# Batch 0 valued by half tiles, low-rank products in pairs, and one batch's keys and queries loaded sooner in a fused attention and mixer kernel

## Chip, cores, metric

The kernel runs on one core of one Trainium2 chip. The metric is the device time of one launch in microseconds (us). The span of a profile is about 1.75 us shorter than the time of the same execution; where milestones are compared below, they count from the start of the span.

## The reference, cut to what matters

```python
# 8 batches, 8 heads, 576 tokens, head size 64; window 64; rank 32
scores = q @ k^T / 8, kept where 0 <= i - j < 64
x = softmax(scores) @ v                        # (8, 576, 512), heads side by side
u = x + (x^T @ U @ V)^T                        # U: 576 x 32, V: 32 x 576, over tokens
out = u + relu(u @ w_ch1) @ w_ch2              # 512 -> 2048 -> 512, "expert products"
```

## The kernel before

The tokens of all batches are cut into nine chunks of 512. A chunk is a list of 32 slots of TensorE work: 16 first products (psA) and 16 quarters of second products (psU), 0.86 us each. The attention of later batches is put between those slots; a table says after which slot each piece comes. Batch 0 has nothing to hide behind, so it runs alone in the first 22 us. From batch 2 on, K and Q are transposed by DMA (`TX`), and each batch's V, K and Q are loaded by DMAs that POOL issues. A copy of one element, `held`, makes POOL wait for an earlier transpose before it issues more.

```python
def PV(t):                                     # batch 0: values of token tile t
    def f():
        xr = ps_big.tile([P, 2, CH], FP32, name="xr", tag="big")
        for h in range(H):
            for blk in blks:
                values(xr[r0 : r0 + W, h // 4, cols], h, blk)
        nc.vector.reciprocal(out=rcp[lo:hi], in_=xv[:, :, :, D:VW])
        nc.vector.tensor_tensor(out=x[lo:hi, t, :, :]..., in0=xv[:, :, :, 0:D], in1=rcp..., op=ALU.mult)
    return f

def UM(ts):                                    # low-rank U product
    for t in ts:
        if t < 4:                              # tile t into column group t
            nc.tensor.matmul(hh["ps"][t * R : (t + 1) * R, :], ub[odd][:, t, :], xt,
                             start=True, stop=False)
            continue
        for g in range(4):                     # last tile, a quarter of the columns to each group
            nc.tensor.matmul(hh["ps"][g * R : (g + 1) * R, cols], ub[odd][:, t, :], xt[:, cols],
                             start=False, stop=True)
    # ... cut: hh["sb"] <- hh["ps"] on ACT

def VM(ts):                                    # low-rank V product, all 128 rows, one per tile
    nc.tensor.matmul(ps[0][:, n, :], vrep[:, off : off + P], hh["sb"][:], start=True, stop=True)
    # ... cut: u = psv + x on DVE, one per tile

def loads(b, *tiles):
    for t in tiles:
        nc.gpsimd.tensor_copy(out=held[:], in_=qfs[(b + 1) % 2][0:1, t * HP * P : t * HP * P + 1])
        if t == tiles[0] and len(tiles) > 1:
            load_v(b + 1)
    for _ in load_kq(b + 2, False):
        pass
# ... cut
if 1 < b and b + 1 < B:
    load_v(b + 1)
# ... cut
slots[20].append(lambda: loads(1, 2, NT - 1))  # hold, V of batch 2, hold, K and Q of batch 3
```

The softmax here doesn't subtract the row's maximum and nothing guards it: scores larger than these inputs give would overflow.

Of the kernel before, what the change touches and what calls it, by code (L numbers as in the profile page):

```python
# [16 lines left out]
def kernel(  # L17
# [11 lines left out]
    nc = tc.nc  # L29
# [192 lines left out]
    def load_rest():  # L222
# [3 lines left out]
        shift_low(0, nc.gpsimd.tensor_copy, 0)  # L226
        for t in range(1, 3):
            shift_low(0, nc.gpsimd.tensor_copy, t)
        load_w1(1024, 2048)
        for g in range(2):  # L230
            spread_v(g, nc.gpsimd.tensor_copy)
# [17 lines left out]
    def attention(b, spare=False):  # L249
# [34 lines left out]
        def TK(j):  # L284
            def f():
                copy = nc.vector.tensor_copy if spare and j == 2 else nc.scalar.copy
                copy(out=place_of(kt, j), in_=tr(kb, j))
            return f

        def TQ(j):  # L290
            def f():
                copy = nc.vector.tensor_copy
                copy(out=place_of(qt, j), in_=tr(qb, j, b == 1))  # L293
            return f
# [114 lines left out]

        def PV(t):  # L410
            def f():
                blks = [bl for bl in (2 * t - odd, 2 * t + 1 - odd) if 0 <= bl < NB]
                lo = W if (odd and t == 0) else 0
                hi = W if (not odd and t == NT - 1) else P

                xr = ps_big.tile([P, 2, CH], FP32, name="xr", tag="big")
                for h in range(H):
                    for blk in blks:
                        r0 = ((blk + odd) % 2) * W
                        cols = slice((h % 4) * VW, (h % 4 + 1) * VW)  # L420
                        values(xr[r0 : r0 + W, h // 4, cols], h, blk)
                xv = xr[lo:hi, :, 0 : 4 * VW].rearrange("p a (h e) -> p a h e", e=VW)
                rcp = wk_pool.tile([P, 2, 4, 1], FP32, name="rcp", tag="rcp")
                nc.vector.reciprocal(out=rcp[lo:hi], in_=xv[:, :, :, D:VW])
                nc.vector.tensor_tensor(
                    out=x[lo:hi, t, :, :].rearrange("p (a h) d -> p a h d", a=2),
                    in0=xv[:, :, :, 0:D],
                    in1=rcp[lo:hi].to_broadcast([hi - lo, 2, 4, D]),
                    op=ALU.mult,
                )  # L430
# [60 lines left out]
        def UM(ts):  # L491
            def f():
# [5 lines left out]
                for t in ts:  # L498
                    xt = x[:, t, :, :].rearrange("p h d -> p (h d)")
                    if t < 4:  # L500
                        nc.tensor.matmul(  # L501
                            hh["ps"][t * R : (t + 1) * R, :], ub[odd][:, t, :], xt,
                            start=True, stop=False,
                        )
                        continue

                    for g in range(4):
                        cols = slice(g * P, (g + 1) * P)
# [47 lines left out]
        def HT(dcs):  # L556
            def f():
                for dc in dcs:
                    nc.tensor.matmul(
                        bank(dc),  # L560
                        hh["sb"][:, dc * P : (dc + 1) * P],
                        vrep[:, W : W + CH],
# [11 lines left out]
        def VM(ts):  # L574
            ps = {}

            def up():
                ps[0] = ps_big.tile([P, 2, CH], FP32, name="psv", tag="big")
                for n, t in enumerate(ts):
                    off = t * P + (0 if odd else W)  # L580
                    nc.tensor.matmul(  # L581
                        ps[0][:, n, :], vrep[:, off : off + P], hh["sb"][:], start=True, stop=True
                    )

            def add(n):
                def f():
                    t = ts[n]
# [3 lines left out]
                    )  # L591
                    if g not in u_tiles:
                        u_tiles[g] = u_pool.tile([P, DM], BF16, name="un")
                    nc.vector.tensor_tensor(  # L594
                        out=u_tiles[g][rs, :],
                        in0=ps[0][rs, n, :],
                        in1=x[rs, t, :, :].rearrange("p h d -> p (h d)"),
# [4 lines left out]
            return [up] + [add(n) for n in range(len(ts))]  # L602
# [26 lines left out]
        pcs["PV"] = [PVA] if not spare else [PV(t) for t in range(NT)]  # L629
        pcs["U"] = [UM((t,)) for t in range(NT)] if spare else [UM(tuple(range(NT)))]  # L630
        if spare:
            pcs["XT"] = [XT(t, range(NDC - 1)) for t in range(NFULL)]
# [4 lines left out]
        else:  # L637
            def whole(ts):
                fs = VM(ts)
                return lambda: [f() for f in fs]  # L640

            pcs["V"] = [whole(ts) for ts in ((0, 1), (2, 3), (4,))]
# [7 lines left out]
    def mlp(c):  # L650
# [3 lines left out]
        def ch1(*ids):  # L654
            def f():
# [5 lines left out]
                for dc in range(NDC):  # L661
# [260 lines left out]
```

## Time and profile before

| | before |
|---|---|
| time, median of the runs at hand when predicting | 313.64 us (313.63 to 318.27) |
| span of the profile | 313.4 us, granted clock 1.00 |
| TensorE busy | 306.1 us |
| first expert product | 21.97 us |
| longest wait of TensorE for a DMA | 1.00 us, before batch 3's scores |

The head of the page of the kernel before. The first line gives busy time, share of the span and instructions of each engine; the others give the busy share in tenths in forty slices of the span.

```profile
PE 306.1 (98%) x2875; PEld 150.9 (48%) x2875; DVE 162.2 (52%) x298; ACT 108.6 (35%) x174; POOL 101.3 (32%) x133
PE   8899999999998999999999999999999999999996
DMA  7999999999999999999999999965100520020012
```

TensorE is never long idle after batch 0. The line of the DMA engines is as full as that of TensorE over the first 25 slices, some 200 us. (It counts the time for which packets are under way; summed over the engines that can exceed 1, so it does not say that no more bytes could pass.)

The list of waits of TensorE, kernel before (engine, line, tile, what it waited for: us in total, times, longest):

```profile
PE low L340 <- DMA qf<-qr: 1.0, 1, 1.0
```

The timeline of SyncE's DMA queue, kernel before: the first and the last of the ten transposing DMAs of batch 3 (start, us of issuing), and the timeline of TensorE at the wait:

```profile
74.62 1.20 SPq L299 DMA_TRANSPOSE kf<-kr  x1
...
89.60 1.37 SPq L299 DMA_TRANSPOSE qf<-qr  x1
```

```profile
93.08 1.03 PE L663 MATMUL psA<-uTc,w1b 128*128 128x512 bf16 x4
...
95.11 0.19 PE L340 MATMUL low<-qf,kf 64*64 64x64 bf16 x1 [1.00 <-DMA qf<-qr]
```

TensorE had finished the slot's expert product by about 94.1 us and stood until the last transposed Q had landed.

The timeline of DVE in batch 0, kernel before: the first and the last of five pairs of reciprocal and multiply.

```profile
15.71 0.21 DVE L424 RECIPROCAL rcp<-xr 128x8 f32<-128x8 f32 x1 [2.34 <-PE xr L402]
15.95 0.69 DVE L425 TENSOR_TENSOR xs<-xr,rcp 128x512 bf16<-128x512 f32 x1
...
19.22 0.20 DVE L424 RECIPROCAL rcp<-xr 64x8 f32<-64x8 f32 x1
19.46 0.68 DVE L425 TENSOR_TENSOR xs<-xr,rcp 64x512 bf16<-64x512 f32 x1
```

Then come ACT's copy of the U product and TensorE's first expert product, kernel before:

```profile
20.48 0.65 ACT L516 CAST hh<-psh 128x256 bf16<-128x256 f32 x2 [1.83 <-PE psh L509]
...
21.97 1.89 PE L663 MATMUL psA<-uTc,w1b 128*128 128x512 bf16 x8
```

The chain of waits of the kernel before, around batch 3's low-rank products (start, us, what). `pshh` is the U product, `psv` the V product.

```profile
110.38 0.33 PE pshh L501 x4
110.71 0.06 PE pshh L509 x4
110.77 0.97 PE psA L663 x4
111.74 0.86 PE psU L687 x4
112.60 0.43 PE psv L581 x2
```

The U product takes 0.39 us. The four expert matmuls behind it take 0.97 us instead of 0.86. Five V products take 5 x 0.216 = 1.08 us.

### The profile page before, as it was taken

Reading aid. Unit: us, or ns where it says so; the run is one execution under the profiler, and the core shown is the slowest. Engines: PE = TensorE matmul, PEld = TensorE weight load, DVE = VectorE, ACT = ScalarE, POOL = GpSimd, SP = SyncE. Lnnn points to the kernel's source line nnn. Section 1 sums busy time; section 2 is a strip of 40 time slices with the busy share of each in tenths; the row PEclk is TensorE's granted clock in tenths of the full one; section 3 lists DMA queues with packets and bytes.
Section 4 is the critical chain, followed back from the end, with each engine's and each line's share of the span. In section 5 each row is a group of like instructions: output and inputs, shape, how many; then the busy total and the mean of one; then the engine's idle time right before and its main releaser. Section 6 shows DMA issues by size and latency. Waiting matters only on the chain.

```text
span 313.4 us, 6904 instructions
## 1 busy us (share of the span) xinstructions
PE 306.1 (98%) x2875; PEld 150.9 (48%) x2875; DVE 162.2 (52%) x298; ACT 108.6 (35%) x174; POOL 101.3 (32%) x133
## 2 busy tenths in 40 slices
PE   8899999999998999999999999999999999999996
PEld 7554554544444544454445444544454444444443
DVE  4475468337756843684358445744574443016011
ACT  3655660467027520533043404440345003301500
POOL 8683263159439346426543571000000000000000
PEclk9999999999999999999999999999999999999999
DMA  7999999999999999999999999965100520020012
GB/s 104 164 208 208 206 168 146 129 180 192 121 153 200 159 152 147 193 140 159 175 174 156 170 156 158 178 99 131 67 2 2 134 84 2 14 86 33 2 61 73
DMA packets 156495, 39.87 MB, mean 127 GB/s; under 512 B 145040, under 2 KB 151440, under 8 KB 156464
## 3 DMA queue, kind: packets, MB, share of 16 engines
q0 software_dynamic: 104720, 18.88, 82.5%
q1 hardware_dynamic: 51744, 20.55, 39.2%
q8 instruction: 22, 0.36, 0.4%
q14 instruction: 9, 0.07, 0.1%
HBM read 37.97 MB, written 9.44 MB: 151 GB/s over the span
## 4 chain that ended last, share of the span: by engine, by line
PE 81%; DMA 13%; POOL 3%; DVE 2%; issue 1%; SPq 0%; POOLq 0%
PE psU L687 36%; PE psA L663 36%; DMA qr<-in_q_dram 4%; DMA vB<-in_v_dram 4%; DMA vA<-in_v_dram 3%; PE psv L581 2%; PE xw L402 2%; PE sc L340 2%; DMA qf<-qr 2%; DVE xs L469 1%; POOL vA L134 1%; PE pshh L501 1%; POOL kr L116 1%; PE tpu L613 0%; POOL vrep L220 0%
## 5 line engine op out<-in xcount | busy, mean ns | idle before, releaser
L687 PE MATMUL psU<-w2b,c 128*128 128x512 bf16 (+2 forms) x592 | 131.3, 373 | 0.1
L663 PE MATMUL psA<-uTc,w1b 128*128 128x512 bf16 x576 | 131.0, 379 | 0.0
L687 PEld LDWEIGHTS <-c 128*128 128x128 bf16 x592 | 56.6, 98 | 64.8 <-issue 0.5
L663 PEld LDWEIGHTS <-w1b 128*128 128x128 bf16 x576 | 54.2, 98 | 64.4 <-issue 1.8
L675 ACT ACTIVATE c<-psA 128x512 bf16<-128x512 f32 x84 | 50.1, 597 | 88.8 <-PE psA L663 88.2
L697 DVE TENSOR_TENSOR osb<-psU,un 128x512 f32<-128x512 f32 (+2 forms) x37 | 24.9, 677 | 76.7 <-PE psU L687 76.3
L673 DVE TENSOR_SCALAR c<-psA 128x512 bf16<-128x512 f32 x60 | 41.3, 689 | 25.5 <-PE psA L663 25.5
L594 DVE TENSOR_TENSOR un<-psv,xs 128x512 bf16<-128x512 f32 (+1 forms) x40 | 25.5, 685 | 22.9 <-PE psv L581 22.7
L134 POOL DMA_DIRECT2D vA<-in_v_dram x32 | 28.6, 909 | 17.3 <-PE psU L687 3.1
L360 ACT ACTIVATE pts<-sc 128x1024 bf16<-128x1024 f32 x32 | 31.3, 1028 | 2.7 <-PE sc L340 2.7
L125 POOL DMA_DIRECT2D kr<-in_k_dram x30 | 25.8, 860 | 10.1 <-DMA vA<-in_v_dram 3.5
L125 POOL DMA_DIRECT2D qr<-in_q_dram x30 | 25.9, 864 | 8.9 <-DMA w2b<-in_moe_w_ch_dram 3.2
L393 ACT ACTIVATE ptl<-low 128x256 bf16<-128x256 f32 x6 | 2.3, 384 | 64.4 <-PE high L340 64.4
L366 DVE TENSOR_TENSOR pts<-pts,maskA 128x1024 bf16<-128x1024 bf16 x28 | 19.1, 682 | 1.1 <-ACT pts L360 1.1
L469 DVE TENSOR_TENSOR xs<-xw,rcw 128x896 bf16<-128x896 f32 x14 | 15.3, 1092 | 0.5
L340 PEld LDWEIGHTS <-kf 64*64 64x64 bf16 x704 | 9.9, 107 | 8.8 <-issue 8.2
L846 POOL COPY held<-qf 1x1 bf16<-1x1 bf16 x6 | 1.1, 178 | 39.4 <-DMA qf<-qr 39.4
L581 PE MATMUL psv<-hh,vrep 128*128 128x512 bf16 x40 | 12.5, 379 | 0.0
L402 PEld LDWEIGHTS <-pts 128*64 128x64 bf16 x512 | 10.0, 110 | 4.7 <-issue 3.7
L340 PE MATMUL sc<-qf,kf 64*64 64x128 bf16 (+1 forms) x608 | 11.6, 212 | 0.6 <-DVE qf L293 0.6
L134 POOL DMA_DIRECT2D vB<-in_v_dram x8 | 7.2, 901 | 5.9 <-DMA qr<-in_q_dram 2.5
L616 ACT COPY uTc<-tpu 128x512 bf16<-128x512 bf16 x9 | 5.3, 586 | 10.8 <-PE tpu L613 10.8
(108 smaller groups left out, 171.2 us busy)
## 6 DMA issues: line engine op xcount, KB each, us to landing
out_dram<-osb SPq DMA_DIRECT2D x35, 256.0 KB, 5.0
vA<-in_v_dram POOLq DMA_DIRECT2D x32, 128.0 KB, 13.1
kr<-in_k_dram POOLq DMA_DIRECT2D x24, 128.0 KB, 8.7
qr<-in_q_dram POOLq DMA_DIRECT2D x24, 128.0 KB, 8.9
w2b<-in_moe_w_ch_dram POOLq DMA_DIRECT2D x4, 512.0 KB, 15.7
vB<-in_v_dram POOLq DMA_DIRECT2D x8, 128.0 KB, 13.7
w1b<-in_moe_w_ch_dram POOLq DMA_DIRECT2D x2, 512.0 KB, 10.9
w1b<-in_moe_w_ch_dram POOLq DMA_DIRECT2D x1, 1024.0 KB, 10.0
```

What stands on the lines that cost most here:

```text
L125: nc.gpsimd.dma_start(out=dst[0:rows, t, :, :], in_=src[b, :, t * P : t * P + rows, :].rearrange("h p d -> p h d"),)
L134: nc.gpsimd.dma_start(out=dst[:, :, 0:D], in_=v[b, :, lo : lo + P, :].rearrange("h p d -> p h d"))
L340: nc.tensor.matmul(sc[g][r0 : r0 + W, col * W : (col + n) * W], keys_of(j, u, rs), queries_of(j, blk, n, rs), start=not spare, stop=last o ...
L360: nc.scalar.activation(out=dst, in_=sc[:], func=ACT.Exp, scale=scale)
L366: nc.vector.tensor_tensor(out=dst, in0=dst, in1=maskA.rearrange("p g n w -> p g (n w)"), op=ALU.mult)
L581: nc.tensor.matmul(ps[0][:, n, :], vrep[:, off : off + P], hh["sb"][:], start=True, stop=True)
L594: nc.vector.tensor_tensor(out=u_tiles[g][rs, :], in0=ps[0][rs, n, :], in1=x[rs, t, :, :].rearrange("p h d -> p (h d)"), op=ALU.add,)
L663: nc.tensor.matmul(ps[i][:], w1b[:, dc, i * P : (i + 1) * P], uTc[:, :, dc, :], start=(dc == 0), stop=(dc == NDC - 1),)
L673: nc.vector.tensor_relu(out=c1[i][:], in_=ps[i][:])
L675: nc.scalar.activation(out=c1[i][:], in_=ps[i][:], func=ACT.Relu)
L687: nc.tensor.matmul(acc[t][:, lo:hi], c1[i][:, t * P : (t + 1) * P], w2b[:, i, lo:hi], start=(i == 0), stop=(i == NFC - 1),)
L697: nc.vector.tensor_tensor(out=osb[:, lo:hi], in0=acc[t][:, lo:hi], in1=u_tiles[g][:, lo:hi], op=ALU.add,)
```

## The change

Its intent: start DVE's chain in batch 0 earlier, by valuing tiles 0 and 1 in head halves as soon as four heads are exponentiated; halve the V products by running them as pairs of 64 rows, for which the U product must fill both halves with the full sum; load and transpose batch 3's K and Q sooner; move batch 1's value products one slot later, with chunk 1's first product split so that it can begin on three of its four tiles. The core of the diff, cuts marked:

```diff
+        def PVL(t):                      # heads 0-3 of tile t
+                half_of(t, 0, xh)
+                scaled(xv, x[:, t, 0:4, :], "h", [4])
+        def PVR():                       # heads 4-7 of tiles 0 and 1
  ... cut: order of batch 0: "... S3 L0 B4 S4 L1", then R, PV2, PV3, PV4
  ... cut: K3's copy moves to DVE, Q2's copy to ACT, two of V's copies to DVE
-                        nc.tensor.matmul(
-                            hh["ps"][t * R : (t + 1) * R, :], ub[odd][:, t, :], xt,
-                            start=True, stop=False,
-                        )
+                        for g in (t % 2, t % 2 + 2):
+                            nc.tensor.matmul(
+                                hh["ps"][g * R : (g + 1) * R, :], ub[odd][:, t, :], xt,
+                                start=(t < 2), stop=False,
+                            )
  ... cut: the last tile fills each group with half the columns instead of a quarter
-                        ps[0][:, n, :], vrep[:, off : off + P], hh["sb"][:], start=True, stop=True
+                        ps[0][n], vrep[half, off : off + P], hh["sb"][half, lo : lo + cols],
+                        start=True, stop=True,
  ... cut: HT in the same pairs; all V products of a batch in one slot
+                parts = (slice(0, TPC - 1), slice(TPC - 1, TPC)) if (c, ids) == (1, (0,)) else (slice(0, TPC),)
  ... cut: batch 1's SV, PV, U, V, UT one slot later, its last V product in slot 31
-        1: {3: [13, 14, 15, 16, 17], 4: [26, 27, 28, 29, 30]},
+        1: {3: [10, 11, 12, 13, 14], 4: [26, 27, 28, 29, 30]},
-                slots[20].append(lambda: loads(1, 2, NT - 1))
+                slots[20].append(lambda: loads(1, 2))
```

More of the change, by code (lines that the diff above doesn't have):

```diff
@@ L220, in spread_v, with load_next @@
         copy(out=vrep[g * R : (g + 1) * R, W : W + S], in_=vf[:])
-    def load_rest():
+    def load_next():
         load_w1(0, 512)
@@ L225, in load_rest @@
         shift_high(0, nc.gpsimd.tensor_copy, 0)
-        shift_low(0, nc.gpsimd.tensor_copy, 0)
-        for t in range(1, 3):
-            shift_low(0, nc.gpsimd.tensor_copy, t)
+        shift_low(0, nc.gpsimd.tensor_copy, 1)
+    def load_rest():
         load_w1(1024, 2048)
-        for g in range(2):
+        for g in range(3):
             spread_v(g, nc.gpsimd.tensor_copy)
@@ L285, in f @@
             def f():
-                copy = nc.vector.tensor_copy if spare and j == 2 else nc.scalar.copy
+                copy = nc.vector.tensor_copy if spare and j >= 2 else nc.scalar.copy
                 copy(out=place_of(kt, j), in_=tr(kb, j))
@@ L291, in f @@
             def f():
-                copy = nc.vector.tensor_copy
+                copy = nc.scalar.copy if spare and j == 2 else nc.vector.tensor_copy
                 copy(out=place_of(qt, j), in_=tr(qb, j, b == 1))
@@ L408, in values, with scaled, half_of, f @@
             )
+        def scaled(src, dst, tag, shape, n=P):
+            rcp = wk_pool.tile([P, *shape, 1], FP32, name="rcp" + tag, tag="rcp" + tag)
+            nc.vector.reciprocal(out=rcp[0:n], in_=src[..., D:VW])
+            nc.vector.tensor_tensor(
+                out=dst,
+                in0=src[..., 0:D],
+                in1=rcp[0:n].to_broadcast([n, *shape, D]),
+                op=ALU.mult,
+            )
+        def half_of(t, a, dst):
+            for h in range(4 * a, 4 * a + 4):
+                for blk in (2 * t, 2 * t + 1):
+                    r0 = (blk % 2) * W
+                    cols = slice((h % 4) * VW, (h % 4 + 1) * VW)
+                    values(dst[r0 : r0 + W, cols], h, blk)
+        def PVL(t):
+            def f():
+                xh = psum["mm"].tile([P, CH], FP32, name="xh", tag="mm")
+                half_of(t, 0, xh)
+                xv = xh[:, 0 : 4 * VW].rearrange("p (h e) -> p h e", e=VW)
+                scaled(xv, x[:, t, 0:4, :], "h", [4])
+            return f
+        def PVR():
+            xr = ps_big.tile([P, 2, CH], FP32, name="xr", tag="big")
+            for t in range(2):
+                half_of(t, 1, xr[:, t, :])
+            xv = xr[:, :, 0 : 4 * VW].rearrange("p t (h e) -> p t h e", e=VW)
+            scaled(xv, x[:, 0:2, 4:8, :], "r", [2, 4])
         def PV(t):
             def f():
-                blks = [bl for bl in (2 * t - odd, 2 * t + 1 - odd) if 0 <= bl < NB]
-                lo = W if (odd and t == 0) else 0
-                hi = W if (not odd and t == NT - 1) else P
+                blks = [bl for bl in (2 * t, 2 * t + 1) if bl < NB]
+                hi = W if t == NT - 1 else P
                 xr = ps_big.tile([P, 2, CH], FP32, name="xr", tag="big")
@@ L418, in f @@
                     for blk in blks:
-                        r0 = ((blk + odd) % 2) * W
+                        r0 = (blk % 2) * W
                         cols = slice((h % 4) * VW, (h % 4 + 1) * VW)
                         values(xr[r0 : r0 + W, h // 4, cols], h, blk)
-                xv = xr[lo:hi, :, 0 : 4 * VW].rearrange("p a (h e) -> p a h e", e=VW)
-                rcp = wk_pool.tile([P, 2, 4, 1], FP32, name="rcp", tag="rcp")
-                nc.vector.reciprocal(out=rcp[lo:hi], in_=xv[:, :, :, D:VW])
-                nc.vector.tensor_tensor(
-                    out=x[lo:hi, t, :, :].rearrange("p (a h) d -> p a h d", a=2),
-                    in0=xv[:, :, :, 0:D],
-                    in1=rcp[lo:hi].to_broadcast([hi - lo, 2, 4, D]),
-                    op=ALU.mult,
-                )
+                xv = xr[0:hi, :, 0 : 4 * VW].rearrange("p a (h e) -> p a h e", e=VW)
+                dst = x[0:hi, t, :, :].rearrange("p (a h) d -> p a h d", a=2)
+                scaled(xv, dst, "r", [2, 4], hi)
             return f
@@ L500, in f @@
                     if t < 4:
-                        nc.tensor.matmul(
-                            hh["ps"][t * R : (t + 1) * R, :], ub[odd][:, t, :], xt,
-                            start=True, stop=False,
-                        )
+                        for g in (t % 2, t % 2 + 2):
+                            nc.tensor.matmul(
+                                hh["ps"][g * R : (g + 1) * R, :], ub[odd][:, t, :], xt,
+                                start=(t < 2), stop=False,
+                            )
                         continue
                     for g in range(4):
-                        cols = slice(g * P, (g + 1) * P)
+                        cols = slice((g % 2) * CH // 2, (g % 2 + 1) * CH // 2)
                         nc.tensor.matmul(
@@ L557, in f @@
             def f():
-                for dc in dcs:
+                for n, dc in enumerate(dcs):
+                    half = slice(n * 2 * R, (n + 1) * 2 * R)
                     nc.tensor.matmul(
                         bank(dc),
-                        hh["sb"][:, dc * P : (dc + 1) * P],
-                        vrep[:, W : W + CH],
+                        hh["sb"][half, dc * P : (dc + 1) * P],
+                        vrep[half, W : W + CH],
                         start=False,
@@ L572, in HT, with VM @@
             return f
-        def VM(ts):
+        def VM(ts, banks=None):
             ps = {}
+            cols = CH if len(ts) == 2 else CH // 2
             def up():
-                ps[0] = ps_big.tile([P, 2, CH], FP32, name="psv", tag="big")
-                for n, t in enumerate(ts):
-                    off = t * P + (0 if odd else W)
+                if banks is None:
+                    pair = ps_big.tile([P, 2, CH], FP32, name="psv", tag="big")
+                    ps[0] = [pair[:, n, 0:cols] for n in range(2)]
+                else:
+                    ps[0] = [one[:, 0:cols] for one in banks()]
+                for n in range(2):
+                    half = slice(n * 2 * R, (n + 1) * 2 * R)
+                    off = ts[n % len(ts)] * P + (0 if odd else W)
+                    lo = 0 if len(ts) == 2 else n * cols
                     nc.tensor.matmul(
-                        ps[0][:, n, :], vrep[:, off : off + P], hh["sb"][:], start=True, stop=True
+                        ps[0][n], vrep[half, off : off + P], hh["sb"][half, lo : lo + cols],
+                        start=True, stop=True,
                     )
@@ L586, in f @@
                 def f():
-                    t = ts[n]
+                    t = ts[n % len(ts)]
                     g = g0 + t
@@ L591, in f @@
                     )
+                    cs = slice(0, CH) if len(ts) == 2 else slice(n * cols, (n + 1) * cols)
                     if g not in u_tiles:
@@ L594, in f @@
                     nc.vector.tensor_tensor(
-                        out=u_tiles[g][rs, :],
-                        in0=ps[0][rs, n, :],
-                        in1=x[rs, t, :, :].rearrange("p h d -> p (h d)"),
+                        out=u_tiles[g][rs, cs],
+                        in0=ps[0][n][rs],
+                        in1=x[rs, t, :, :].rearrange("p h d -> p (h d)")[:, cs],
                         op=ALU.add,
@@ L600, in add @@
                 return f
-            return [up] + [add(n) for n in range(len(ts))]
+            return [up, add(0), add(1)]
         def UT(t):
@@ L628, in attention @@
             pcs["M"].insert(0 if b >= NGR else HP, MK8)
-        pcs["PV"] = [PVA] if not spare else [PV(t) for t in range(NT)]
+        pcs["PV"] = [PVA] if not spare else [None, None] + [PV(t) for t in range(2, NT)]
         pcs["U"] = [UM((t,)) for t in range(NT)] if spare else [UM(tuple(range(NT)))]
         if spare:
+            pcs["L"] = [PVL(t) for t in range(2)]
+            pcs["R"] = PVR
             pcs["XT"] = [XT(t, range(NDC - 1)) for t in range(NFULL)]
@@ L637, in attention, with two_banks, mixed, last @@
         else:
-            def whole(ts):
-                fs = VM(ts)
-                return lambda: [f() for f in fs]
-            pcs["V"] = [whole(ts) for ts in ((0, 1), (2, 3), (4,))]
+            def two_banks():
+                return (
+                    psum["mm"].tile([P, CH], FP32, name="psv0", tag="mm"),
+                    ps_tp.tile([P, CH], FP32, name="psv1", tag="tp"),
+                )
+            def mixed(parts=None):
+                parts = parts or [VM((NT - 1,), two_banks), VM((0, 1)), VM((2, 3))]
+                for part in parts:
+                    part[0]()
+                for part in parts:
+                    for add in part[1:]:
+                        add()
+            pcs["V"] = [mixed]
+            if b == 1:
+                def last():
+                    for f in VM((NT - 1,)):
+                        f()
+                pcs["V"] = [lambda: mixed([VM((0, 1)), VM((2, 3))]), last]
             pcs["UT"] = [UT(t) for t in range(NT if odd else NT - 1)]
@@ L660, in f @@
                     ps = {i: pair[:, n, :] for n, i in enumerate(ids)}
-                for dc in range(NDC):
-                    for i in ids:
-                        nc.tensor.matmul(
-                            ps[i][:],
-                            w1b[:, dc, i * P : (i + 1) * P],
-                            uTc[:, :, dc, :],
-                            start=(dc == 0),
-                            stop=(dc == NDC - 1),
-                        )
+                parts = (slice(0, TPC - 1), slice(TPC - 1, TPC)) if (c, ids) == (1, (0,)) else (slice(0, TPC),)
+                for ts in parts:
+                    for dc in range(NDC):
+                        for i in ids:
+                            nc.tensor.matmul(
+                                ps[i][:, ts.start * P : ts.stop * P],
+                                w1b[:, dc, i * P : (i + 1) * P],
+                                uTc[:, ts, dc, :],
+                                start=(dc == 0),
+                                stop=(dc == NDC - 1),
+                            )
                 for i in ids:
@@ L708, in mlp @@
             ups[0:2] = [ch1(0, 1), lambda: None]
-            return ups + [ch2(t, r) for u in (0, 2) for r in range(4) for t in (u, u + 1)]
+            rest = [ch2(t, r) for r in range(4) for t in (0, 1)]
+            return ups + rest + [ch2(t, r) for t in (2, 3) for r in range(4)]
         rest = [ch2(t, r) for t in range(TPC) for r in range(4)]
@@ L720 @@
         "U": [14],
-        "V": [16, 17, 18],
+        "V": [16],
         "UT": [17, 17, 18, 18, 19],
     }
-    PLACE_0 = {"V": [0, 0, 1, 2, 2, 3, 4, 4]}
+    PLACE_0 = {"V": [0, 0, 1, 2, 2, 3, 4, 4, 4]}
     PLACE_1 = {
@@ L728 @@
         "M": [13, 14, 16, 17, 17],
-        "SV": [17, 17, 18, 18],
-        "PV": [19],
-        "U": [24],
-        "V": [25, 26, 27],
-        "UT": [27, 28, 29, 30, 102],
+        "SV": [18, 18, 19, 19],
+        "PV": [20],
+        "U": [25],
+        "V": [26, 31],
+        "UT": [28, 29, 30, 31, 102],
     }
@@ L740 @@
         "U": [23],
-        "V": [24, 25, 26],
+        "V": [24],
         "UT": [27, 28, 29, 30],
@@ L790 @@
     repeat(nc.scalar.copy, maskB)
-    order = "K0 K1 B0 B1 Q0 Q1 S0 K2 S1 K3 B2 Q2 Q3 S2 B3 S3 B4 S4"
+    load_next()
+    order = "K0 K1 B0 B1 Q0 Q1 S0 K2 S1 K3 B2 Q2 Q3 S2 B3 S3 L0 B4 S4 L1"
     for what in order.split():
         j = int(what[1])
-        if what[0] in "SB":
+        if what == "L1":
+            shift_low(0, nc.vector.tensor_copy, 0)
+            shift_high(0, nc.vector.tensor_copy, 1)
+        if what[0] in "SBL":
             a[what[0]][j]()
@@ L803 @@
     load_rest()
-    for t in range(NT + 2):
-        if t < NT:
-            a["PV"][t]()
-        if t < 2:
-            shift_high(0, nc.scalar.copy, t + 1)
-        elif 3 <= t < NT:
-            spread_v(t - 1, nc.scalar.copy)
-        if 2 <= t < NFULL + 2:
-            a["XT"][t - 2]()
-            a["U"][t - 2]()
-        elif t == 1:
-            a["idle"](1)
+    a["R"]()
+    shift_high(0, nc.scalar.copy, 2)
+    shift_low(0, nc.scalar.copy, 2)
+    a["idle"](1)
+    a["PV"][2]()
+    spread_v(3, nc.scalar.copy)
+    a["XT"][0]()
+    a["XT"][1]()
+    a["PV"][3]()
+    a["U"][0]()
+    a["PV"][4]()
+    a["U"][1]()
+    for t in range(2, NFULL):
+        a["XT"][t]()
+        a["U"][t]()
     load_low_rank_1()
@@ L849, in loads @@
                     )
-                    if t == tiles[0] and len(tiles) > 1:
-                        load_v(b + 1)
+                if b == 1:
+                    load_v(b + 1)
                 for _ in load_kq(b + 2, False):
```

## The prediction

> **What bounds it now.** The page has TensorE busy 306.1 of 313.4 us at full granted clock (DVE 52%, ACT 35%). The two expert products (psA, psU) are 262 us of that; in the chain of waits twelve 128x512 matmuls take 2.59 us, 0.216 each. TensorE's idle time, from the table of stretches: 2.8 us before 20 us (where much else is filler or latency), 0.1 in 40-50, 1.0 in 80-100, 3.1 in the tail, nearly none elsewhere.
>
> **1. Batch 3's K/Q sooner: -1.0 us.** The list of waits shows TensorE waiting 1.00 us, until 95.1, for the last transposing DMA of batch 3's Q. Its loads are held to 69.06 us by the second "held" copy; the transposes start at 74.62. The change drops that copy, so loads follow V (about 65.7 us), and transposes may start about 3 us sooner. That covers a wait of one, unless the nearly full DMA queues land everything no sooner.
>
> **2. Batch 0: -0.4 us.** The timeline shows DVE as the chain: five reciprocal + multiply pairs (0.20 + 0.69 us) from 15.71 to 20.14 us; the first expert product starts at 21.97. DVE idles 13.4-15.7. Two half tiles (estimate 0.55 us each) can start near 14.1. But DVE also takes two 0.3 us copies of V, and halves pay fixed cost again. My schedule ends tile 4 at about 19.7 instead of 20.14. K3 on DVE and Q2 on ACT bring S2 forward 0.1 us.
>
> **3. Paired low-rank products: 0 (-0.5 to +0.5).** Now the five V products take 5 x 0.216 = 1.08 us per batch, without a change of array shape. As 64-row pairs they need 0.54 us, but the array changes shape and back. The Trainium skill, "TensorEngine Tiling (Array Packing)", Key Properties, says that changing the tiling mode drains TensorE. This trace agrees: the four matmuls after the U product take 0.97 instead of 0.86 us, and its four column tiles 0.33 instead of 0.216: 0.22 us there and back. So 0.76 us: -0.3 per batch. The U product, though, must fill both copies: eight 512-wide and four 256-wide matmuls, two passes for one, +0.26 us. Net about -0.05 for each later batch. Batch 0 pays the shape change three times, batch 1 twice: +0.1 each. The paired products that end batch 0 aren't on the path: the first expert product waits for the first ACT copy.
>
> **4. Batch 1 and chunk 1: -0.2 us.** Batch 1's value products take 1.83 us (45.14 to 46.97) against 1.3 for batch 2, because the last V tile lands at 46.4. One slot later takes about 0.4 off. The transposes move a slot later too, so chunk 1's first product would wait for the last copy: transposes to use takes 0.86 us, its three ready tiles cover 0.65: +0.2 us.
>
> Sum: -1.6 us. **Predicted 312.0 us, 8 in 10 within 310.8 to 313.2.** Chances: over 2% faster 0.01, within 2% 0.98, slower 0.01.
>
> **What would show it.** 1: no wait for batch 3's transposes near 92 us. 2: first psA near 21.5 us; DVE's first multiply near 14.3. 3: V products as one group of six, near 0.65 us, then a longer next group; U near 0.65 us instead of 0.39. 4: batch 1's value products 1.3-1.4 us; a short idle in chunk 1's first product. From 100 to 310 us at most 0.5 us shorter.
>
> **What would make it wrong.** Row pairs that don't overlap (+2 us in all); cheaper shape changes between row pairs and the full array (-1); DMA moved earlier delaying V; six adds behind one group delaying psU's evacuations.

## The result, and the profile after

| | before | changed |
|---|---|---|
| median | 313.7 us (6 runs, 313.23 to 318.27) | 313.46 us (6 runs, 313.29 to 314.69) |
| ratio of fast runs, 95% interval | | 1.0000 (0.9977 to 1.0023) |
| span of the profile | 313.4 us | 312.9 us |

A ratio here is the mean time of one kernel's fast runs over that of the other's of the same rounds, so it isn't quite the ratio of the medians. (A run over 1.5% above the fastest of its kernel, as the one of 318.27 us, isn't counted as fast.) The predicted 312.0 us (310.8 to 313.2) lies below what was measured: the change does nothing that can be told from chance.

The same places in the profile after. The list of waits and TensorE's timeline before batch 3's scores:

```profile
PE low L340 <- DMA qf<-qr: 1.1, 1, 1.1
```

```profile
92.74 1.03 PE L719 MATMUL psA<-uTc,w1b 128*128 128x512 bf16 x4
...
94.91 0.19 PE L340 MATMUL low<-qf,kf 64*64 64x64 bf16 x1 [1.15 <-DMA qf<-qr]
```

SyncE's queue, changed kernel, first and last transposing DMA of batch 3:

```profile
73.09 1.57 SPq L299 DMA_TRANSPOSE kf<-kr  x1
...
88.88 1.90 SPq L299 DMA_TRANSPOSE qf<-qr  x1
```

The wait that the first term of the prediction was to remove is still there. POOL issued batch 3's first load 4.8 us sooner (64.25 instead of 69.06), the first transpose came only 1.5 us sooner, the last was issued 0.7 us sooner, and the scores started 0.2 us sooner.

DVE's timeline in batch 0, changed kernel, the first multiply and the last, and then ACT's copy of the U product and TensorE's first expert product, for which the lines before have 20.48 and 21.97:

```profile
14.41 0.42 DVE L413 TENSOR_TENSOR xs<-xh,rcph 128x256 bf16<-128x256 f32 x1
...
19.12 0.68 DVE L413 TENSOR_TENSOR xs<-xr,rcpr 64x512 bf16<-64x512 f32 x1
```

```profile
20.39 0.65 ACT L541 CAST hh<-psh 128x256 bf16<-128x256 f32 x2 [2.79 <-PE psh L534]
...
21.87 1.89 PE L719 MATMUL psA<-uTc,w1b 128*128 128x512 bf16 x8 [0.40 <-ACT uTc L594]
```

DVE is done at 19.80 instead of 20.14 us, as predicted (19.7). But from there to ACT's copy it now takes 0.59 us instead of 0.34, so only 0.1 of the 0.34 us is left at the first product.

The chain of waits, changed kernel, batch 3's low-rank products:

```profile
110.21 0.55 PE pshh L526 x8
110.75 0.11 PE pshh L534 x4
110.86 0.97 PE psA L719 x4
...
112.70 0.65 PE psv L614 x6
```

The row pairs overlap: six products take 0.65 us. The U product takes 0.66 us instead of 0.39. With 0.11 us behind the V products, for the array's return to full shape, both together take 1.42 us instead of 1.47. That fits the Trainium skill, "TensorEngine Tiling (Array Packing)", Key Properties, by which a change of tiling mode drains TensorE; the trace shows the 0.11 us, not what fills it.

Where does the time go? TensorE's work is the same in each execution of a kernel, so the milestones of several executions can be set side by side. The table gives the time of the first expert product, then the distances to chunk 1's first product, to the scores of batches 2, 3, 4 and 7, and to the end, each from the milestone in the row above, read from TensorE's timelines. The columns other than the first and third are experiments told below.

| stretch, us | before | before again (e13) | changed | changed (e5) | changed (e18) | before, fewer loads (e15) | changed, fewer loads (e16) |
|---|---|---|---|---|---|---|---|
| to first expert product | 21.97 | 22.10 | 21.87 | 22.33 | 21.92 | 22.49 | 22.77 |
| to chunk 1 | 37.89 | 37.79 | 37.52 | 37.51 | 37.52 | 37.42 | 37.51 |
| to batch 2's scores | 8.95 | 8.95 | 9.14 | 9.14 | 9.14 | 8.95 | 9.15 |
| to batch 3's scores | 26.30 | 25.35 | 26.38 | 25.17 | 25.17 | 25.22 | 25.16 |
| to batch 4's scores | 32.31 | 32.09 | 32.28 | 32.19 | 32.04 | 32.10 | 32.05 |
| to batch 7's scores | 96.30 | 96.30 | 96.13 | 96.13 | 96.13 | 96.30 | 96.13 |
| to the end | 89.68 | 89.62 | 89.58 | 89.63 | 89.58 | 89.62 | 89.63 |
| span | 313.4 | 312.2 | 312.9 | 312.1 | 311.5 | 312.1 | 312.4 |

The first row varies by itself: in kernels with the changed batch 0 it lies between 21.87 and 22.77 us here, and was 23.25 us in e10 and 25.08 us in e19, each with a wait of TensorE of 1.6 us for a load of Q at the start. So one profile's span can't show a gain of 1.6 us.

### The profile page after: what moved, and what is told of

It is laid out like the page before. It is cut to its first block, busy times and chain, and to the rows that moved or that the text cites. A ratio compares the mean times of both kernels' runs of the same rounds, so it can differ in the third digit from the quotient of the medians.

```text
span 312.9 us, 6984 instructions
## 1 busy us (share of the span) xinstructions
PE 303.1 (97%) x2897; PEld 147.4 (47%) x2919; DVE 163.4 (52%) x310; ACT 108.7 (35%) x173; POOL 100.4 (32%) x131
## 4 chain that ended last, share of the span: by engine, by line
PE 92%; DMA 3%; DVE 2%; issue 1%; ACT 1%; SPq 0%; POOLq 0%
PE psA L719 39%; PE psU L743 39%; PE sc L340 3%; PE xw L402 2%; DMA qf<-qr 2%; PE psv L614 2%; DMA kr<-in_k_dram 2%; PE pshh L526 1%; PE tpg L276 1%; DVE c L729 1%; PE sc L330 1%; DVE xs L413 0%; PE tpu L648 0%; PE tpm L276 0%; PE low L340 0%
## 5 line engine op out<-in xcount | busy, mean ns | idle before, releaser
L719 PE MATMUL psA<-uTc,w1b 128*128 128x512 bf16 (+1 forms) x580 | 131.2, 379 | 0.4 <-ACT uTc L594 0.4
L743 PE MATMUL psU<-w2b,c 128*128 128x512 bf16 (+2 forms) x572 | 127.5, 374 | 1.3 <-issue 0.3
L629 DVE TENSOR_TENSOR un<-psv,xs 128x512 bf16<-128x512 f32 (+3 forms) x48 | 26.1, 592 | 23.4 <-PE psv L614 23.2
L134 POOL DMA_DIRECT2D vA<-in_v_dram x32 | 28.3, 892 | 17.7 <-DMA kr<-in_k_dram 3.1
L493 DVE TENSOR_TENSOR xs<-xw,rcw 128x896 bf16<-128x896 f32 x14 | 15.3, 1091 | 0.5
L541 ACT CAST hh<-pshh 128x512 bf16<-128x512 f32 x7 | 4.1, 585 | 13.7 <-PE pshh L534 13.5
```

The source lines that it names most:

```text
L134: nc.gpsimd.dma_start(out=dst[:, :, 0:D], in_=v[b, :, lo : lo + P, :].rearrange("h p d -> p h d"))
L629: nc.vector.tensor_tensor(out=u_tiles[g][rs, cs], in0=ps[0][n][rs], in1=x[rs, t, :, :].rearrange("p h d -> p (h d)")[:, cs], op=ALU.add,)
L719: nc.tensor.matmul(ps[i][:, ts.start * P : ts.stop * P], w1b[:, dc, i * P : (i + 1) * P], uTc[:, ts, dc, :], start=(dc == 0), stop=(dc == ...
L743: nc.tensor.matmul(acc[t][:, lo:hi], c1[i][:, t * P : (t + 1) * P], w2b[:, i, lo:hi], start=(i == 0), stop=(i == NFC - 1),)
```

## The experiments

The first theory (A in the expectations): batch 3's last transposing DMA sets the clock, so all that TensorE gains before 94 us is absorbed in that wait. Its rival (B): TensorE's work counts everywhere. Each run is timed beside the kernel before on the same chip; ratios are to that. There is no e14; e5, e13, e17, e18 and e19 run a kernel again.

### e1: four idle matmuls in chunk 1, slot 20

```diff
+ slots[20]: fl = ps_tp.tile(...); four matmuls idle x idle, 512 wide, into fl
```

> The changed kernel with four idle 512-wide matmuls (0.86 us of TensorE) added in chunk 1, after slot 20, about 79 us. Theory A (batch 3's transposing DMA sets the clock: whatever TensorE gains or loses before its wait near 94 us is absorbed there): the wait before batch 3's scores shrinks from 1.1 to about 0.2 us, the scores still start at 94.9 +- 0.3 us, and the total changes by less than 0.3 us. Rival B (TensorE work counts everywhere, the wait is a fixed delay that follows TensorE): wait stays near 1.1 us, scores start near 95.8, total +0.86 us.

Ratio 1.0109 (1.0082 to 1.0136), median 318.74 us. This was a mistake of mine: the PSUM bank was still being read by DVE. TensorE's timeline of e1:

```profile
79.35 1.90 PE L743 MATMUL psU<-w2b,c 128*128 128x512 bf16 x8
83.56 1.85 PE L957 MATMUL fill<-idle 128*128 128x512 bf16 x4 [2.31 <-DVE xs L505]
```

The stretches of e1 (us, TensorE busy with its instructions, granted clock, DMA share, GB/s):

```profile
82.00:83.00 1.00, 0.00 (x0) 1.00 1.78 155
83.00:84.00 1.00, 0.44 (x2) 0.82 2.34 162
84.00:85.00 1.00, 1.00 (x4) 0.50 2.16 72
```

After 2.3 us of idleness the granted clock fell to half for some 3 us, so four matmuls cost over 4 us. Batch 3's scores started at 98.98 us without a wait. The run doesn't test A against B; e9 does it again.

### e2: batch 3's scores two slots later

```diff
-    PLACE_3 = {**PLACE, "SV": [5, 5, 6, 6]}
+    PLACE_3 = {"S": [2, 2, 2, 5, 5], "M": [2, 3, 4, 6, 7], "SV": [5, 5, 6, 6], "PV": [10], "U": [16], "V": [18], "UT": [19, 19, 20, 20, 21]}
```

> The changed kernel with batch 3's scores and all that follows from them placed two slots (1.7 us of expert product) later. Theory A: TensorE finds expert products to do while the last transposing DMA of batch 3 lands at about 94.8 us, the wait of 1.1 us is gone and the total falls by 0.7 to 1.1 us (312.3 to 312.8). Rival B (the wait only moves, because ACT and DVE then have too little time for batch 3's exponentials and masks before its value products): a wait of similar size appears before the value or the U product of batch 3, total within 0.3 us of the change.

Ratio 1.0131 (1.0104 to 1.0158): both expectations missed. The wait before the scores was gone, but the list of waits of e2 has a new one:

```profile
PE psA L719 <- DMA uTc<-un: 4.2, 1, 4.2
```

That is chunk 3 waiting for the DMA that transposes batch 3's u, which had moved later with the rest. Again the clock dropped behind it (granted 0.50 from 128 to 134 us). DMA has little slack there too.

### e3: batch 3's V after its transposes

```diff
-            if 1 < b and b + 1 < B:
+            if 2 < b and b + 1 < B:
                 load_v(b + 1)
-                if b == 1:
+                if b <= 2:
                     load_v(b + 1)          # behind the wait for batch 3's middle transpose
```

> The changed kernel with batch 3's V loads issued after the wait for batch 3's middle transpose (about 91 us) instead of at 76 us, so that they don't share the DMA queues with batch 3's transposes. Theory C (the transposes are slowed by the loads of V beside them): the ten transposes, issued from 73.1 to 90.8 us in the change, take at least 2 us less, the wait of 1.1 us is gone or under 0.3 us; V may then come late for batch 3's value products at 104 us. Rival D (the transposes are paced by themselves or by the landing of K and Q): the last is issued within 0.5 us of 88.9 and the wait stays about 1.1 us.

The wait was gone, but so it was without this edit in e5, told next but one. What the edit shows is the length of the transposes. SyncE's queue of e3, first and last transpose of batch 3:

```profile
72.79 1.21 SPq L299 DMA_TRANSPOSE kf<-kr  x1
...
86.09 1.23 SPq L299 DMA_TRANSPOSE qf<-qr  x1
```

The ten were issued in 14.5 us (72.79 to 87.32) instead of 17.7 (73.09 to 90.78). So V's loads beside the transposes do lengthen them: the three profiles with V later (e3, e6, e8) have 14.2 to 14.5 us, the profiles with V beside them 15.4 to 17.7. This agrees with the Trainium skill, "DMA: Bandwidth & Descriptors", Issuing engines are not separate DMA queues: DMAs of all issuing engines run on the same sixteen DMA engines and interleave. The time: ratio 0.9982 (0.9958 to 1.0006), not told from 1. TensorE reached chunk 3 with 0.1 us of wait, so the next DMA was just in time.

### e4: batch 3's K and Q ahead of batch 2's V

```diff
-                if b == 1:
-                    load_v(b + 1)
                 for _ in load_kq(b + 2, False):
                     pass
+                if b == 1:
+                    load_v(b + 1)
```

> The changed kernel with batch 3's K and Q loaded ahead of batch 2's V instead of behind it in the same queue. Theory D (K and Q land late because they queue behind V: first load issued 4.8 us sooner in the change, first transpose only 1.5 us sooner): the first transpose is issued at about 69 to 70 us (slot 10) instead of 73.1, the last about 3 us sooner, and the wait of 1.1 us at batch 3's scores is gone; batch 2's V comes some us later and may stall its value products at 78 us by up to 2 us. Rival (transposes paced by themselves): first transpose sooner, last not, wait unchanged.

Ratio 1.0368 (1.0324 to 1.0413). The first transpose was issued at 65.67 us, even sooner than expected, so K and Q had indeed queued behind V. But batch 2's value products then waited for V, by the list of waits 3.9 us in three waits for DVE's copies of V and 4.5 us in two for V itself, mostly at half clock (granted 0.50 from 82 to 94 us). What one load gains in this queue, another loses.

### e5: the changed kernel again

> The changed kernel itself again, beside the next three on the same chip. Both theories: 313 to 315 us, within 0.4 us of the kernel before on this chip; its profile again shows a wait of about 1 us at batch 3's scores, the scores starting at 94.9 +- 0.5 us.

Ratio 1.0003 (0.9982 to 1.0024). Its profile missed the expectation: no wait before batch 3's scores. TensorE's timeline of e5:

```profile
93.19 1.03 PE L719 MATMUL psA<-uTc,w1b 128*128 128x512 bf16 x4
...
94.15 0.21 PE L340 MATMUL low<-qf,kf 64*64 64x64 bf16 x1
```

So theory A as stated fell: the wait isn't in every execution of the changed kernel. The new theory (L): which DMA is late, and by how much, differs from execution to execution, by as much as the change was to gain.

### e6: the kernel before, batch 3's V later

The same move as e3, in the kernel before.

> The kernel BEFORE with one edit only: batch 3's V loads issued after the wait for batch 3's middle transpose instead of beside its transposes. Theory C (V's loads beside the transposes set their end): the ten transposes take about 14.5 us from first to last issue instead of 16.3, the wait of 1.0 us before batch 3's scores is gone or under 0.3 us, and the total falls by 0.7 to 1.0 us without anything of the change. Rival (the sooner loads of the change were needed as well): the wait stays over 0.5 us because the transposes still start at 74.6.

Ratio 1.0044 (1.0018 to 1.0070): 0.4% slower, clear of noise, against both. The transposes took 14.2 us and the wait before the scores was gone, as theory C said (in e13 it was gone without any edit), but chunk 3 now waited 1.0 us for the transposed u. In this profile the stretch to chunk 1, which the edit doesn't touch, was longer too (38.35 us), because a V tile of batch 1 was late; so how much of the 0.4% is the edit's is open. The list of waits of e6:

```profile
PE psA L663 <- DMA uTc<-un: 1.0, 1, 1.0
```

### e7: later batches unpaired

```diff
-                        for g in (t % 2, t % 2 + 2):
+                        for g in (t % 2, t % 2 + 2) if spare else (t,):
-                    half = slice(n * 2 * R, (n + 1) * 2 * R)
+                    half = slice(n * 2 * R, (n + 1) * 2 * R) if spare else slice(0, P)
 ... cut: the last tile's columns and the start flag likewise
```

> The changed kernel with the low-rank products of batches 1 to 7 unpaired again (four U products into four column groups, V products over all 128 rows), their places kept. Costing from the traces: U group 0.39 us instead of 0.66, V group 1.08 instead of 0.65 with no longer group behind it: from one batch's scores to the next's +0.06 to +0.10 us, five batches after the wait near 94 us, so total +0.2 to +0.5 us; batches 1 and 2 lie before that wait and count nothing. Rival (pairing is what gains or loses here): over 0.8 us either way.

Ratio 1.0006 (0.9980 to 1.0032), not told from e5's 1.0003, so the timed runs don't test the expected 0.2 to 0.5 us. The chain of waits of e7, batch 3:

```profile
109.28 0.33 PE pshh L526 x4
109.61 0.06 PE pshh L534 x4
...
111.50 1.08 PE psv L614 x6
```

Batches 4 to 7 took 96.31 us instead of 96.13, so a pair gains 0.06 us per batch. Up to chunk 1 the unpaired kernel took 37.36 us instead of 37.51: in batch 1, where the V products come in two groups, pairing costs 0.15 us.

### e8: three edits together

```diff
 ... as e3, and in batch 0:
-    for t in range(2, NFULL):
-        a["XT"][t]()
-        a["U"][t]()
+    for t in range(2, NFULL):
+        a["XT"][t]()
+    for t in range(2, NFULL):
+        a["U"][t]()
 ... and uT's first two copies each split between ACT and DVE
```

> The changed kernel with batch 3's V later (as e3), batch 0's transposes of tiles 2 and 3 put together before their U products, and the first two uT copies split between ACT and DVE. Front: hh's first copy about 20.15 us instead of 20.39, first psA about 21.4 instead of 21.87. If TensorE is the only limit then the total is 1.4 to 1.6 us below the change (about 312). Theory A says the next DMA landing (batch 3's transposed u at about 125 us, which e3 met with 0.1 us to spare) takes back most of the front's 0.5 us: a wait of 0.2 to 0.6 us near 125 us, total about 0.9 to 1.2 us below the change.

Ratio 0.9998 (0.9972 to 1.0023): nothing. From tile 4 valued to ACT's copy it took 0.40 us instead of 0.59, but the split copies made it worse: copy to first product 1.73 us instead of 1.48, because DVE's half waited for ACT's. In this profile the second half of Q landed late at the start (first product at 23.45 us), which hid the rest. From batch 3's scores to batch 4's it took 32.35 us, 0.3 more than in e18: about the wait near 125 us that theory A had named.

### e9, e10: idle matmuls early and late

```diff
+ e9:  chunk 1, slot 16: four idle matmuls, 512 wide, 0.86 us
+ e10: chunk 4, slot 24: the same
```

> The changed kernel with four idle 512-wide matmuls (0.86 us) after slot 16 of chunk 1, where their bank is free (e1 put them where the bank was still being read, which stalled TensorE for over 2 us and lowered its clock). Theory A: S of batch 3 still starts at 94.9 +- 0.4 us, the wait before it shrinks from 1.1 to about 0.2 us, total within 0.3 us of the change. Rival B: total +0.86 us.

> The same four idle matmuls after slot 24 of chunk 4 (about 185 us), past the last wait of TensorE for a DMA. Both theories: full price, total +0.8 to +1.0 us over the change, no wait changed. If it cost nothing, there would be slack that this reading doesn't know.

Ratios 1.0009 (0.9994 to 1.0024) and 1.0033 (1.0012 to 1.0053), medians 314.31 and 315.38 us. In e9's profile the scores started at 94.90 us without a wait, but 26.03 us after batch 2's, 0.86 more than in e5: full price, in an execution that wouldn't have waited. In e10 the stretch with the filler took 32.90 us instead of 32.04: full price too. The timed runs hint that the early filler is partly absorbed, but the two intervals overlap, so that stays open.

### e11: only the order of batch 0's last products

The second edit of e8 alone.

> The changed kernel with only the order of batch 0's last products changed: transposes of tiles 2 and 3 together, then their U products together, so that the array changes shape once instead of three times before the last U product. If alternating shapes is what ate the gain of the DVE chain (tile 4 valued 0.34 us sooner, hh's copy only 0.09): hh's first copy at about 20.15 us instead of 20.39, first psA about 21.63 instead of 21.87. Rival (the fill of the U product's second pass itself): under 0.1 us. Total within 0.3 us of the change either way, since the wait near 94 us absorbs it.

Ratio 1.0010 (0.9981 to 1.0039). Inconclusive: the copy came at 20.27 us, 0.72 us after tile 4, because one U product stood 0.2 us with no visible cause. e8, with the same order, had 0.40. So the alternation of shapes is a likely cause of the lost 0.25 us, not a shown one. Its wait before batch 3's scores was 0.4 us, a third value.

### e12, e17: the change without its K/Q part

```diff
-                slots[20].append(lambda: loads(1, 2))
+                slots[20].append(lambda: loads(1, 2, NT - 1))
-        1: {3: [10, 11, 12, 13, 14], ...
+        1: {3: [13, 14, 15, 16, 17], ...
 ... cut: load_v after the first hold, as before
```

> The changed kernel with its K/Q part undone (second hold back, transposes three slots later). The part was worth 1.0 us in the prediction; the traces say that it moved the last landing by 0.2 us. Reading from the traces: first transpose back at 74.3, scores of batch 3 at 95.0 to 95.2, total +0.1 to +0.3 us. Rival (the part prevents a longer wait, since TensorE now comes 0.3 us sooner): wait 1.3 us or more, total +0.4 to +1.0.

> e12 again with five rounds, to see whether the change without its K/Q part is really 0.2% below the kernel before (e12: 0.9983, interval 0.9968 to 0.9998). Theory L: 0.997 to 1.001, not to be told from the change itself (1.0000 and 1.0003); if below 0.9985 again, the K/Q part does harm.

Ratios 0.9983 (0.9968 to 0.9998) and 0.9971 (0.9951 to 0.9992), and no wait before batch 3's scores in either profile. Both expectations of e12 missed: they had it slower than the change, and its scores came at 93.75 us. By the words of e17's expectation the part does harm; e18 and e19 compare it on one chip.

### e13: the kernel before again

> The kernel before, profiled again. Theory L (which DMA is missed, and by how much, differs from execution to execution; the wait of 1.0 us before batch 3's scores is not in every execution of the kernel before, as it was in one of two profiles of the change): wait between 0 and 1.3 us, span between 311.5 and 313.5 us, the span moving with the waits for DMA. Theory A as first stated (the wait is in every execution): 1.0 +- 0.2 us again.

One look: 313.93 us, span 312.2. TensorE's timeline of e13, the kernel before:

```profile
93.11 1.03 PE L663 MATMUL psA<-uTc,w1b 128*128 128x512 bf16 x4
...
94.19 0.19 PE L340 MATMUL low<-qf,kf 64*64 64x64 bf16 x1
```

No wait. TensorE came to the scores at the same moment as in the first profile (the expert product ahead of them began at 93.11 us, in the first profile at 93.08), but the last transposed Q was there: its DMA had been issued at 88.48 us instead of 89.60. The 1.00 us of the first profile was a property of that execution.

### e15, e16: both kernels with fewer loads

```diff
     def load_v(b):
+        if b >= 2:
+            return
     def load_kq(b, split):
+        if b >= 4:
+            return
```

Their outputs are wrong, which doesn't matter for the times.

> The kernel before without the loads of V from batch 2 on and of K and Q from batch 4 on (wrong results on purpose: older data are used again), so that no DMA is late past 60 us. Together with e16 it shows what the change is worth to TensorE alone. No wait before batch 3's scores nor at chunk 3's start; from the start of chunk 1 to the end as in the profile of before less its waits: total 1.0 to 1.5 us below the kernel before if the wait is in most executions, 0.3 to 0.8 if it is in half.

> The changed kernel with the same loads left out. Summed from the profiles without DMA waits: first product -0.1 us, batch 1's value products and pairs up to chunk 1 -0.37, chunk 1's first product in parts +0.19, batches 2 to 7 -0.05 to -0.06 each: 0.5 to 0.7 us below e15. If it is 1.2 us or more below, the prediction's sum was right and only DMA hid it; if it is within 0.2 us, TensorE itself gained nothing.

Ratios to the whole kernel before: 0.9977 (0.9953 to 1.0000) and 0.9967 (0.9945 to 0.9990); medians 313.32 and 313.38 us. So with no late DMA in the middle, both kernels are 0.2 to 0.3% faster (for e15 the interval just reaches 1), and alike. For e15 that is 0.73 us by the medians, in the range expected if half of the executions wait. The expected 0.5 to 0.7 us between them did not come. From the first expert product on, the two profiles took 289.61 and 289.63 us (span less first product): TensorE's gains and costs cancel. The transposes of batch 3 took 15.3 us in e15 and 19.2 us in e16, without any V beside them, but began 3 to 8 us sooner; so V's loads are not all that sets their length.

### e18, e19: with and without the K/Q part on one chip

> The changed kernel, beside the same kernel with its K/Q part undone (e19) on one chip. Theory L (the K/Q part neither gains nor costs; what is read is which execution waits): both ratios to the kernel before between 0.996 and 1.001 and within 0.0015 of each other. Theory H (the K/Q part costs what the rest gains): this one 0.999 to 1.001, e19 0.0015 to 0.003 below it. A wait before batch 3's scores in this profile would be the third in four profiles of the change or, if absent, the second without.

> As e18, without the K/Q part. Theory L: within 0.0015 of e18. Theory H: ratio 0.997 to 0.9985 again and 0.0015 to 0.003 below e18; no wait before batch 3's scores, as in e12 and e17.

Ratios 0.9987 (0.9947 to 1.0027) and 0.9985 (0.9942 to 1.0028): alike, as theory L had it. But each interval is over 1 us wide to either side, so this pair alone rules out neither a gain nor a cost of 1 us. With e5 and e12, e17 it says more: with the part the ratios were 1.0000, 1.0003 and 0.9987, without it 0.9983, 0.9971 and 0.9985. A gain of 1.0 us would put the first three 0.003 below the others; none lies below any of them. Whether the part costs 0.1 to 0.2% stays open. No wait in either profile. In e19's, the second half of Q landed so late at the start that the granted clock fell to half there, and the span was 314.7 us; e18's was 311.5.

## Why the prediction was wrong, point by point

**1. K/Q sooner, -1.0 us: this is the step that failed.** "The list of waits shows TensorE waiting 1.00 us" was true of one execution and was taken as a property of the kernel. The kernel before waited 1.00 us in one profile and not at all in the next (e13). The changed kernel waited 1.15 us, and not at all in e5 and e18. Without its K/Q part it did not wait in three profiles. By the ratios of all six runs the part gains no 1 us (see e18, e19). The prediction's own doubt was right for the profile that it read: loads issued 4.8 us sooner ended in scores 0.2 us sooner, because K and Q queue behind V (e4) and because the transposes are lengthened by V's loads beside them (e3, e6).

The profiles whose edits leave these loads and the clock alone show the same without leaning on one wait. Counted from chunk 1's first product, the first of the ten transposes was issued after 12.7 to 13.7 us in the seven profiles with the part (changed, e5, e7, e9, e10, e11, e18) and after 13.3 to 14.8 us in four without it (before, e12, e13, e17; e19 began 3 us late), the last after 27.7 to 29.5 and after 27.4 to 29.7 us. So the part starts the transposes about 1 us sooner, they take longer (16.5 to 17.7 against 15.4 to 16.4 us), and the last comes no sooner. Its scores waited in two of the seven (1.15 and 0.42 us), and in one of the five without it (1.00 us).

**2. Batch 0, -0.4 us: right for DVE, wrong for the path.** Tile 4 was valued at 19.80, 20.26 and 19.86 us in the changed kernel and at 20.14 and 20.27 in the kernel before. In two of the three the chain gained what was predicted; in the third (e5) DVE's copy of a V tile in that chain took 0.76 us, in e18 0.29. But the stretch from there to ACT's copy grew from 0.34 to 0.58 or 0.59 us in each of the three changed profiles. I had the U product's second pass in the sum for later batches and left it out here, where it stands on the path. How much of the 0.25 us is that pass, and how much the order of transposes and U products, isn't shown: with the other order the stretch was 0.40 us in e8 and 0.72 in e11. At the first expert product: 21.87, 22.33 and 21.92 against 21.97 and 22.10. No gain that stands out of the spread.

**3. Paired products, 0: right.** Predicted -0.05 per later batch and +0.1 for batch 1; measured -0.06 and +0.15 (e7). Its +0.1 us for batch 0 wasn't measured apart from the 0.25 us of point 2.

**4. Batch 1 and chunk 1, -0.2: half right.** The +0.2 us of the first product in parts is there in each changed profile (9.14 against 8.95). The -0.4 of the later value products depends on V's landing: against the two profiles of the kernel before it is about -0.3 with pairing's cost included (37.52 against 37.79 and 37.89); where V landed in time (e15, 37.42) it is +0.1.

So the sum for TensorE is not -1.6 but about zero when no DMA is late (e15 against e16), and -0.5 from the first product on in e18 against e13 (289.58 against 290.10), where batch 1's V was late in the kernel before; 0.27 of it lies before chunk 1. Spans of one and the same kernel spread over more than that: 312.1 to 313.6 us in e5's six runs. The measured ratios of the change, 1.0000, 1.0003 and 0.9987, fit. What makes the landing of a DMA vary by a microsecond between executions is not settled here, nor is the share of executions that wait. No version tried beats both kernels by more than chance: without the K/Q part was 0.2 to 0.3% below the kernel before in e12 and e17, but not below the change beside it in e19.

## What to carry to other kernels

A wait for a DMA of about 1 us in one profile is a sample; where the DMA engines are nearly full, look at a second execution before a term of a sum rests on it. Where the DMA queue was full, an earlier or later issue mostly changed who waits (e2, e4, e6): name the transfer that will now be later. And when a change adds work to an engine that was off the path, add it once more at the place where that engine comes onto the path.

## What the Trainium skill lacked or had wrong

- "TensorE: Matmul & The Clock Gate", Part 1, has the clock return to half after at least one idle window of about 3.4 us, and its section on oscillation warns of gaps above that. In e1 a gap of 2.3 us was followed by a granted clock of 0.50, and in e19 one of 1.6 us, at the start; a gap of 1.6 us in e10 was not. So shorter gaps can cost the clock, and not always.
- "TensorEngine Tiling (Array Packing)" says that a mode change drains TensorE but not what it costs: here about 0.11 us on the way in (0.33 us for four U products side by side, against 0.216 for one) and 0.11 us on the way back (0.97 against 0.86 us for the next four expert matmuls). It has no measured gain of 64-row pairs: six products in pairs did in 0.65 us what five over all rows did in 1.08.
- "DMA: Bandwidth & Descriptors" says that all DMAs share the engines, but gives no measure of how a transposing stream suffers beside loads: ten transposes were issued in 14.2 to 14.5 us with V's loads moved behind them (e3, e6, e8) and in 15.4 to 17.7 us with V's loads beside them.
- No page that I read has how much landings differ between executions of one program: the same transposed Q of the changed kernel was 1.15 us late in one execution and in time in two others.
